# Splitting the first batch's attention into two groups of heads at the start of an attention and feed-forward kernel, with later places for the work behind it

## The chip, the cores and the metric

The kernel runs on one core of a Trainium2 chip. The metric is the device time of one execution in microseconds (us). The kernel before took 573.24 us (median of three runs, 572.38 to 573.35). "TensorE", "VectorE", "ScalarE" are PE, DVE, ACT in the profile; POOL and SP issue the transfers. The kernel's matmuls write to eight PSUM banks, pA0 to pA3 and pF0 to pF3 (pA and pF in the profile).

## The reference

Linformer attention (8 batches, 8 heads, 1024 positions, head size 64), whose keys and values are first projected to 64 rows, then a gated feed-forward part on the 8192 rows that come out.

```python
def _attn_ref(q, k, v, E, F):
    k_proj = np.einsum('ks,bhsd->bhkd', E, k)
    v_proj = np.einsum('ks,bhsd->bhkd', F, v)
    scores = (1.0 / np.sqrt(q.shape[-1])) * np.matmul(q, k_proj.transpose(0, 1, 3, 2))
    # ... softmax over the 64 projected keys ...
    return np.matmul(attn, v_proj)

def _moe_ref(x, w_gate, w_val, w_out):          # x: 8192 x 512
    gate = 1.0 / (1.0 + np.exp(-(x @ w_gate)))   # 512 x 1536
    return gate * (x @ w_val) @ w_out            # 1536 x 512
```

## The kernel before

A small planner (`Plan`) turns the tiles that each operation reads and writes into semaphores. A PSUM bank is one key that every user writes, so any two engines on one bank take turns. `Ring` hands out banks in turn: `whole` has pA0 to pA3 and pF0 to pF2 (used only at the start), `att` pA0 to pA3, `ffn` pF0 to pF3. `mm` is a matmul, `act` a ScalarE operation, `dve` a VectorE one, `busy(n)` issues n small matmuls that only keep TensorE at work ("filler"). Of the tiles, `qT` holds the transposed queries, `kp` and `kpD` the projected keys, `vpD` the projected values, `xT` the attention's output, `hT` the gated values and `ost` the rows on their way out.

The softmax is turned round: exps `eT`, their sums by matmul, a reciprocal on VectorE, a split into two bf16 parts (`rhl`), a broadcast of these by matmul (`bc`, copied to `rb`), and the unnormalised output product (`xo`) multiplied by `rb` into `xT`:

```python
def den():                                   # sums of exps, then VectorE
    bk = ring.next()
    for n in range(4):
        for c in range(4):
            mm(bk, bank[bk][32 * n : 32 * n + 32, 0:P], dsel8[:, n % 2, c, :],
               eT[:, n, c * P : (c + 1) * P], ...)          # (arguments cut)
    dve(lambda e: e.reciprocal(rden[:, 0:P], bank[bk][:, 0:P]), [], [("rden", 0)], b=bk)
    dve(lambda e: e.tensor_copy(rhi[:, 0:P], rden[:, 0:P]), ...)
    dve(lambda e: e.scalar_tensor_tensor(rhl[:, 0:P], ...), ...)
```

The start, on half of batch 0's positions (512 of 1024 make one feed-forward block, and `R` is a group of four heads):

```python
busy(56)
bk = whole.next()
project(0, 0, [bk, bk], 0)          # K
keep_k(bk, 0)
turn_k(whole)
qt, sc, den, bc, xo = half_unit(0, whole)
qt(0); qt(1); sc(0); sc(1)          # (one statement to a line in the kernel)
den()
bks = [whole.next(), whole.next()]
project(1, 1, bks, 0)               # V
keep_v(bks, 0, ["ACT", "DVE", "ACT", "DVE"])
busy(8); bc(0); busy(4); xo(0); bc(1); xo(1); busy(10)
```

Then comes the stream. A block has 12 feed-forward steps (four gate and four value matmuls of 512 columns, then a tanh on ScalarE and `hT` on VectorE), and output products of the block before stand in "gaps". "Step i" below is a place in this list; the first place of block 0 holds the pair of steps 0 and 1. Attention work of later blocks is put into places with `put`:

```python
if blk == 1:
    gaps = {7: [0], 9: [1], 11: [2, 3]}      # output products of block 0
# ...
if b == 0:
    qt, sc, den, bc, xo = half_unit(1, att)  # second half of batch 0
    put(1, lambda: (qt(0), qt(1)))
    put(2, lambda: sc(0))
    put(4, lambda: sc(1))
    put(5, den)
    put(7, lambda: (bc(0), xo(0)))
    put(9, lambda: (bc(1), xo(1)))
    spots = (14, 15, 18, 19, 20, 20, 22, 23, 24, 25)   # attention of batch 1
```

The softmax here doesn't subtract the row's maximum and nothing guards it: scores larger than these inputs give would overflow.

Of the kernel before, what the change touches and what calls it, by code (L numbers as in the profile page):

```python
# [7 lines left out]
ALU = mybir.AluOpType  # L8
# [110 lines left out]
def bass_linformer_attn__then__ffn_glu_sigmoid_kernel(  # L119
# [18 lines left out]
    with contextlib.ExitStack() as es:  # L138
# [94 lines left out]
        def load_k(b):  # L233
            n = 2 * b % 3
            load(
                KV[n][:, :, :],
                k[b].rearrange("h (p t) d -> p h (t d)", t=NT),
                [("KV", n)],
                f"KV{n}",
                r=turned(b - 1) if b >= 2 else (),  # L240
            )

        def load_v(b):
            n = (2 * b + 1) % 3
            load(
                KV[n][:, :, :],
                v[b].rearrange("h (p t) d -> p h (t d)", t=NT),
                [("KV", n)],
                f"KV{n}",
            )  # L250

        def load_q(b):
            s = b % 2
            load(
                Qb[s][:, :, :],
                q[b].rearrange("h (p t) d -> p h (t d)", t=NT),
                [("Q", s, 0), ("Q", s, 1)],
                f"Q{s}",
            )

        def load_q_half(b, hf):
            s, cc = b % 2, slice(256 * hf, 256 * hf + 256)
            load(
                Qb[s][:, :, cc],
                q[b].rearrange("h (p t) d -> p h (t d)", t=NT)[:, :, cc],
                [("Q", s, hf)],
                f"Q{s}{hf}",
            )

        WCH = (0, 256, 512, 1024, 1536)  # L270

        def load_w(j):
            c = slice(WCH[j], WCH[j + 1])
            load(wG[:, :, c], wg_v[:, :, c], [("wG", j)], f"wG{j}")
            load(wV[:, :, c], wv_v[:, :, c], [("wV", j)], f"wV{j}")


        def start_loads():
            for src, rows, n in ((E, slice(0, 64), "E"), (F, slice(64, 128), "F")):
                add(  # L280
                    "SP",
                    lambda e, src=src, rows=rows: e.dma_start(EF[rows, :], src[:, :]),
                    w=[("EF", n)],
                    dma="in" + n,
                )
            for i in range(4):
                pool(
                    lambda e, i=i: e.memset(quad[32 * i : 32 * i + 32, :], 32.0 * i),
                    w=[("quad", i)],
                )  # L290
            load_k(0)
            load_q_half(0, 0)
            load_v(0)
            load_w(0)
            load_w(1)
            load_q_half(0, 1)
            load_w(2)
            load_w(3)

# [119 lines left out]
        def project(n, w, bks, c0):  # L419
            src = KV[n][:, :, :].rearrange("p (r h) (t d) -> p h t r d", h=2, t=NT)  # L420
            for t in range(NT):
                for h in range(2):
                    mm(
                        bks[h],
                        bank[bks[h]][64 * h : 64 * h + 64, c0 : c0 + 256],
                        EFT[:, t, 64 * w : 64 * w + 64],
                        src[:, h, t, :, :],
                        [("KV", n), ("EFT", t // 4)],
# [5 lines left out]
        def keep_k(bk, c0):  # L434
            act(kp[:, :, :], bank[bk][:, c0 : c0 + 256], [], ["kp"], b=bk)

        def keep_v(bks, c0, engines):
            vv = vpD[:, :, :].rearrange("p (r h) d -> p r h d", h=2)
            for n, (h, g) in enumerate(((0, 0), (1, 1), (0, 1), (1, 0))):
                o = vv[64 * g : 64 * g + 64, :, h, :]  # L440
                i = bank[bks[h]][64 * h : 64 * h + 64, c0 : c0 + 256].rearrange(
                    "p (r d) -> p r d", r=NR
                )
                if engines[n] == "ACT":
                    act(o, i, [], [("vpD", h, g)], b=bks[h])
                else:
                    dve(lambda e, o=o, i=i: e.tensor_copy(o, i), [], [("vpD", h, g)], b=bks[h])

        def turn_k(ring):
            bk = ring.next()  # L450
            ob = bank[bk][:, :].bitcast(BF16)
            for r in range(NR):
                for g in range(2):
                    mm(
                        bk,
                        ob[64 * g : 64 * g + 64, r * P : (r + 1) * P],
                        kp[:, r, :],
                        ident[:, :],
                        ["kp", "ident"],
# [4 lines left out]
                kpD[:, :, :].rearrange("p h c -> p (h c)"), ob[:, 0:512], [], ["kpD"], b=bk  # L464
            )

        VPD = [("vpD", h, g) for h in range(2) for g in range(2)]

        def half_unit(hf, ring):
# [4 lines left out]
            def qt(R):  # L474
                bk = ring.next()
                ob = bank[bk][:, :].bitcast(BF16)
                for x in range(4):
                    for t in range(2):
# [6 lines left out]
                            [("Q", s, hf), "ident"],  # L485
# [4 lines left out]
                if R == 0:  # L490
                    dve(lambda e: e.tensor_copy(o, i), [], [("qT", s, hf, R)], b=bk)
                else:
                    act(o, i, [], [("qT", s, hf, R)], b=bk)

            def sc(R):
                bks = [ring.next(), ring.next()]
                for rr in range(2):
                    for c in range(2):
                        h = 4 * R + 2 * rr + c
                        for g in range(2):  # L500
# [6 lines left out]
                                ["kpD", ("qT", s, hf, R)],  # L507
# [13 lines left out]
            def den():  # L521
                bk = ring.next()
                for n in range(4):
                    for c in range(4):
# [11 lines left out]
                    lambda e: e.reciprocal(rden[:, 0:P], bank[bk][:, 0:P]),  # L536
                    [],
                    [("rden", 0)],
# [3 lines left out]
                    lambda e: e.tensor_copy(rhi[:, 0:P], rden[:, 0:P]), [("rden", 0)], ["rhi"]  # L542
# [3 lines left out]
                        rhl[:, 0:P], rhi[:, 0:P], rows[:, 3, 0:1], rden[:, 0:P], ALU.mult, ALU.add  # L546
                    ),
                    [("rden", 0), "rhi", "rows"],
                    ["rhl"],
                )  # L550

            def bc(R):
                bks = [ring.next(), ring.next()]
                for c in range(4):
                    for g in range(2):
# [7 lines left out]
                            ["bsel8", "rhl"],  # L563
# [7 lines left out]
            def xo(R):  # L571
                bks = [ring.next(), ring.next()]
                for rr in range(2):
                    for g in range(2):
                        for c in range(2):
# [7 lines left out]
                                VPD + [("eT", 2 * R + g)],  # L583
# [18 lines left out]
        def transpose_q(b):  # L602
            s = b % 2
            for r in range(NR):
# [6 lines left out]
                    r=[("Q", s, 0), ("Q", s, 1)],  # L611
                    w=[("qT", s, r), ("qT", s, 0, r // 2), ("qT", s, 1, r // 2)],
# [3 lines left out]
        def attention(b):  # L616
            s = b % 2

            def kv():
# [7 lines left out]
                for t in range(NT):  # L627
                    for w in range(2):
# [7 lines left out]
                            [("KV", n), ("EFT", t // 4)],  # L636
# [14 lines left out]
                for g in range(2):  # L651
# [4 lines left out]
                        [("vpD", h, g) for h in range(2)],  # L656
# [3 lines left out]
            def turn_kd():  # L660
                if b == 1:
# [9 lines left out]
                    w=["kpD"],  # L671
# [3 lines left out]
            def sc(r2):  # L675
                for r in (2 * r2, 2 * r2 + 1):
                    bks = [att.next(), att.next()]
                    for c in range(2):
                        h = 2 * r + c
                        for g in range(2):  # L680
# [6 lines left out]
                                ["kpD", ("qT", s, r)],  # L687
# [13 lines left out]
            def den():  # L701
# [14 lines left out]
                for c in range(4):  # L716
# [4 lines left out]
                        [("rden", c)],  # L721
# [3 lines left out]
            def split():  # L725
                rd = [("rden", c) for c in range(4)]
                dve(lambda e: e.tensor_copy(rhi[:, :], rden[:, :]), rd, ["rhi"])  # L727
# [4 lines left out]
                    rd + ["rhi", "rows"],  # L732
                    ["rhl"],
                )

            def bc(rnd):
                for j in range(4):
# [6 lines left out]
                        ["bsel", "rhl"],  # L744
# [4 lines left out]
            def gather():  # L749
                for i in range(4):  # L750
# [3 lines left out]
                        r=[("rden", c) for c in range(4)],  # L754
# [16 lines left out]
            def xo(r2):  # L771
                for r in (2 * r2, 2 * r2 + 1):
                    bks = [att.next(), att.next()]
                    for g in range(2):
                        n = 2 * r + g
                        for c in range(2):
# [6 lines left out]
                                VPD + [("eT", n)],  # L783
# [32 lines left out]
        def msteps(blk, ms):  # L816
            s, hf = (blk // 2) % 2, blk % 2
            pbs = {}
            for m in ms:
                for n in "GV":  # L820
                    pbs[m, n] = ffn.next()
            for i in range(NI):
                for m in ms:
                    j = max(x for x in range(4) if WCH[x] <= m * P)
                    for n, W in (("G", wG), ("V", wV)):
                        if len(ms) > 1:
                            mm_one(blk, m, j, i, n, W, pbs[m, n], s, hf)
            if len(ms) == 1:
                m = ms[0]
                j = max(x for x in range(4) if WCH[x] <= m * P)  # L830
                for n, W in (("G", wG), ("V", wV)):
                    for i in range(NI):
                        mm_one(blk, m, j, i, n, W, pbs[m, n], s, hf)
            for m in ms:
                gate(blk, m, pbs[m, "G"], pbs[m, "V"])

        def mm_one(blk, m, j, i, n, W, pb, s, hf):
# [5 lines left out]
                [("w" + n, j), ("xT", s, i, hf, 0), ("xT", s, i, hf, 1)],  # L843
# [55 lines left out]
        busy(56)  # L899
        bk = whole.next()  # L900
        project(0, 0, [bk, bk], 0)
        keep_k(bk, 0)
        turn_k(whole)
        qt, sc, den, bc, xo = half_unit(0, whole)
        qt(0)
        qt(1)
        sc(0)
        sc(1)
        den()
        bks = [whole.next(), whole.next()]  # L910
        project(1, 1, bks, 0)
        keep_v(bks, 0, ["ACT", "DVE", "ACT", "DVE"])
        busy(8)
        bc(0)
        busy(4)
        xo(0)
        bc(1)
        xo(1)
        busy(10)
# [4 lines left out]
        load(wO[:, :, :], moe_w_out.rearrange("(m p) c -> p m c", p=P), ["wO"], "wO")  # L924
# [7 lines left out]
        for b in range(B):  # L932
            todo = []
            for blk in (2 * b, 2 * b + 1):
# [3 lines left out]
                if blk == 1:  # L938
                    gaps = {7: [0], 9: [1], 11: [2, 3]}
                else:  # L940
                    gaps = {2: [0], 5: [1], 8: [2], 11: [3]}
                for m in ms:
                    todo.append(lambda blk=blk, m=m: msteps(blk, m))
# [8 lines left out]
            if b == 0:  # L952
                qt, sc, den, bc, xo = half_unit(1, att)
                put(1, lambda: (qt(0), qt(1)))
                put(2, lambda: sc(0))
                put(4, lambda: sc(1))
                put(5, den)
                put(7, lambda: (bc(0), xo(0)))
                put(9, lambda: (bc(1), xo(1)))
                spots = (14, 15, 18, 19, 20, 20, 22, 23, 24, 25)  # L960
# [10 lines left out]
            if b == 0:  # L971
                put(3, lambda: transpose_q(1))
                put(15, lambda: load_next(2))
# [43 lines left out]
```

## Time and profile before

The time is fixed by when the steady stream of feed-forward matmuls starts and by each later moment at which TensorE waits (it is busy for 97% of the span). So I cut the trace of the kernel before at four points, all starts of TensorE groups in the timeline:

| point | start, us |
|---|---|
| the mark: gate matmuls of the third step of block 0 | 29.38 |
| first gate matmuls of block 1 (B1G) | 50.46 |
| first value matmuls of block 1 (B1V) | 51.33 |
| first gate matmuls of block 2 (B2) | 89.97 |
| span | 570.5 |

After B2 the programs are the same, so a difference of two kernels is the sum of the differences of these stretches.

### The profile page before, as it was taken

Reading aid. Unit: us, or ns where it says so; the run is one execution under the profiler, and the core shown is the slowest. Engines: PE = TensorE matmul, PEld = TensorE weight load, DVE = VectorE, ACT = ScalarE, POOL = GpSimd, SP = SyncE. Lnnn points to the kernel's source line nnn. Section 1 sums busy time; section 2 is a strip of 40 time slices with the busy share of each in tenths; the row PEclk is TensorE's granted clock in tenths of the full one; section 3 lists DMA queues with packets and bytes.
Section 4 is the critical chain, followed back from the end, with each engine's and each line's share of the span. In section 5 each row is a group of like instructions: output and inputs, shape, how many; then the busy total and the mean of one; then the engine's idle time right before and its main releaser. Section 6 shows DMA issues by size and latency. Waiting matters only on the chain.

```text
span 570.5 us, 7585 instructions
## 1 busy us (share of the span) xinstructions
PE 552.1 (97%) x2960; PEld 248.6 (44%) x3014; DVE 247.8 (43%) x392; ACT 175.7 (31%) x305; POOL 100.4 (18%) x138
## 2 busy tenths in 40 slices
PE   5799999999999999999999999999999999999997
PEld 5444434444444444444444444444444444444443
DVE  4345265334633536235543355334462354533332
ACT  2454551442233322342123422243213332222220
POOL 8100010106300081002700044000700007000000
PEclk9999999999999999999999999999999999999999
DMA  9999899984755059521687037660411101010012
GB/s 160 200 207 201 121 185 147 182 159 77 139 112 98 33 113 165 98 61 51 109 158 120 19 79 126 133 102 37 80 52 47 37 22 39 37 38 27 30 37 92
DMA packets 74212, 56.00 MB, mean 98 GB/s; under 512 B 34528, under 2 KB 65760, under 8 KB 74176
## 3 DMA queue, kind: packets, MB, share of 16 engines
q0 software_dynamic: 31776, 29.89, 34.3%
q1 hardware_dynamic: 42400, 25.63, 18.3%
q8 instruction: 23, 0.38, 0.3%
q14 instruction: 13, 0.11, 0.1%
HBM read 60.29 MB, written 16.78 MB: 135 GB/s over the span
## 4 chain that ended last, share of the span: by engine, by line
PE 85%; DMA 10%; POOL 2%; DVE 1%; issue 1%; SPq 0%; ACT 0%; DVEq 0%; POOLq 0%
PE pF L210 78%; PE pA L210 7%; DMA Qb<-in_q_dram 6%; DMA qT<-Qb 4%; DVE rden L719 1%; POOL wG L228 1%; POOL wV L228 1%; POOL KV L228 0%; POOL Qb L228 0%; SPq L607 0%; DVE rhl L729 0%; DVE ost L882 0%; DVE hT L855 0%; ACT sig L214 0%; DVE rhi L727 0%
## 5 line engine op out<-in xcount | busy, mean ns | idle before, releaser
L855 DVE SCALAR_TENSOR_TENSOR hT<-sig,pF 128x512 bf16<-128x512 f32 x192 | 130.6, 685 | 203.5 <-PE pF L210 153.5
L214 ACT ACTIVATE sig<-pF 128x512 f32<-128x512 f32 x192 | 114.3, 599 | 315.7 <-PE pF L210 312.8
L210 PE MATMUL pF<-xT,wV 128*128 128x512 bf16 x754 | 196.7, 379 | 1.6 <-DVE xT L589 0.9
L210 PE MATMUL pF<-xT,wG 128*128 128x512 bf16 x747 | 194.5, 379 | 2.3 <-issue 1.4
L210 PE MATMUL pF<-wO,hT 128*128 128x512 bf16 x702 | 163.5, 379 | 1.5 <-issue 0.8
L210 PEld LDWEIGHTS pF<-xT,wV 128*128 128x128 bf16 x768 | 75.2, 98 | 90.8 <-issue 0.6
L210 PEld LDWEIGHTS pF<-xT,wG 128*128 128x128 bf16 x768 | 72.2, 98 | 95.3 <-issue 12.9
L764 POOL PARTITION_BROADCAST rb<-rrow x96 | 70.8, 798 | 212.8 <-DMA rrow<-rden 207.7
L210 PEld LDWEIGHTS pF<-wO,hT 128*128 128x128 bf16 x720 | 69.3, 98 | 87.2 <-issue 5.8
L882 DVE TENSOR_SCALAR ost<-pF 128x512 f32<-128x512 f32 x60 | 41.5, 691 | 94.0 <-PE pF L210 94.0
L214 ACT ACTIVATE eT<-pA 128x512 bf16<-128x512 f32 x63 | 32.7, 603 | 10.2 <-PE pA L210 10.2
L789 DVE TENSOR_TENSOR xT<-pA,rb 128x512 bf16<-128x512 f32 x56 | 34.7, 681 | 0.0
L719 DVE RECIPROCAL rden<-pA 128x128 f32<-128x128 f32 x28 | 23.7, 910 | 0.0
L228 POOL DMA_DIRECT2D KV<-in_k_dram x8 | 7.3, 918 | 87.9 <-PE pA L210 56.3
L228 POOL DMA_DIRECT2D KV<-in_v_dram x8 | 7.1, 882 | 80.5 <-PE pF L210 79.1
L214 ACT ACTIVATE kpd<-pA 64x1024 bf16<-64x1024 f32 x6 | 6.1, 1017 | 28.3 <-PE pA L210 28.3
L210 PE MATMUL pA<-KV,EFT 128*64 128x512 bf16 (+1 forms) x144 | 14.5, 346 | 0.0
L210 PE MATMUL pA<-qT,kpD 64*64 64x512 bf16 (+1 forms) x140 | 10.6, 367 | 0.4 <-ACT qT L214 0.3
L210 PE MATMUL pA<-wO,hT 128*128 128x512 bf16 x47 | 10.5, 379 | 0.1
L210 PE MATMUL pA<-eT,vpD 64*64 64x512 bf16 (+1 forms) x136 | 10.4, 370 | 0.0
L210 PEld LDWEIGHTS pA<-KV,EFT 128*64 128x64 bf16 x144 | 7.4, 109 | 6.8 <-issue 3.0
L214 ACT ACTIVATE rb<-pA 128x512 f32<-128x512 f32 x14 | 7.5, 617 | 4.9 <-PE pA L210 4.9
(67 smaller groups left out, 104.4 us busy)
## 6 DMA issues: line engine op xcount, KB each, us to landing
out_dram<-ost SPq DMA_DIRECT2D x64, 256.0 KB, 2.0
KV<-in_k_dram POOLq DMA_DIRECT2D x8, 1024.0 KB, 10.4
KV<-in_v_dram POOLq DMA_DIRECT2D x8, 1024.0 KB, 14.6
Qb<-in_q_dram POOLq DMA_DIRECT2D x7, 1024.0 KB, 15.0
wO<-in_moe_w_out_dram POOLq DMA_DIRECT2D x1, 1536.0 KB, 49.6
Qb<-in_q_dram POOLq DMA_DIRECT2D x2, 512.0 KB, 17.1
wG<-in_moe_w_gate_dram POOLq DMA_DIRECT2D x2, 512.0 KB, 25.2
wV<-in_moe_w_val_dram POOLq DMA_DIRECT2D x2, 512.0 KB, 27.0
```

Of the source, the lines that this page charges most:

```text
L210: return add("PE", lambda e: e.matmul(o, lhsT, rhs, **kw), r=r, x=[("bank", b)])
L214: return add("ACT", lambda e: e.activation(o, i, func, scale=scale), r=r, w=w, x=x)
L228: add("POOL", lambda e: e.dma_start(o, i), r=r, w=w, dma=sem)
L719: lambda e, cc=cc: e.reciprocal(rden[:, cc], bank[bk][:, cc]),
L764: lambda e, n=n, i=2 * rnd + c, j=j, parts=parts: e.partition_broadcast(rb[0:parts, n, :], rrow[32 * j : 32 * j + 1, i, :], channels=parts),
L789: lambda e, r=r, g=g, n=n, bk=bks[g]: e.tensor_tensor(xT[s][:, r, :, 256 * g : 256 * g + 256], bank[bk][:, :].rearrange("p (f c) -> p f c" ...
L855: lambda e: e.scalar_tensor_tensor(hT[blk % 2][:, m, :], sg[:, :], 1.0, bank[pv][:, :], ALU.add, ALU.mult,),
L882: lambda e: e.tensor_scalar(o[:, :], bank[pb][:, :], 0.5, None, op0=ALU.mult),
```

## The change

Its intent is to begin sooner: load K, Q and V of batch 0 by groups of four heads, and finish the first group's attention and half of the first feed-forward pair while the second group is still on its way. With it go later places for the second half of batch 0 and for batch 1, all output products of block 0 at the end of block 1, and a wait of the output weights' load for the transposed queries of batch 1. Core of the diff:

```diff
-            load_k(0)
-            load_q_half(0, 0)
-            load_v(0)
-            load_w(0)
+            for R in range(2):
+                load_kv_heads(0, k, R)
+            for R in range(2):
+                load_q_half(0, 0, R)
+            for R in range(2):
+                load_kv_heads(1, v, R)
+            load_w(0, 0)
+            load_w(0, 1)
 ... (weights in more, smaller pieces; keys by group of heads; den, sc, xo per group)
-        busy(56)
 ... (the start as shown above)
+        busy(40)
 ... (one line: half_unit)
+        for R in range(2):
+            bk = whole.next()
+            project(0, 0, [bk, bk], 0, R)
+            busy(4)
+            keep_k(bk, 0, R)
+            turn_k(whole, R)
+            busy(8)
+        qt(0, ("DVE", "ACT"))
+        busy(6)
+        sc(0)
+        qt(1, ("DVE", "DVE"))
+        busy(6)
+        den(0)
+        sc(1)
+        busy(4)
 ... (v_part(R, ring): the V projection of group R on two banks of the ring, and its copies to vpD)
+        bc(0)
+        den(1)
+        v_part(0, whole)
+        busy(4)
+        bc(1)
+        xo(0)
+        busy(8)
+        for _ in range(-att.turn % 4):
+            att.next()
+        v_part(1, att)
 ... (first pair: matmuls i=0,1 of step 0, then xo(1), i=0,1 of step 1, then i=2,3)
+        transpose_q(1)
         load(wO ...
+            r=turned(1),
-                    gaps = {7: [0], 9: [1], 11: [2, 3]}
+                    gaps = {11: [0, 1, 2, 3]}
-                put(1, lambda: (qt(0), qt(1)))
 ... (places 1, 2, 4, 5, 7, 9 as shown above)
+                put(5, lambda: (qt(0, ("DVE", "ACT")), qt(1, ("DVE", "ACT"))))
+                put(6, lambda: sc(0))
+                put(7, lambda: (den(0), sc(1)))
+                put(8, lambda: (den(1), bc(0)))
+                put(9, lambda: (xo(0), bc(1)))
+                put(10, lambda: xo(1))
-                spots = (14, 15, 18, 19, 20, 20, 22, 23, 24, 25)
+                spots = (16, 17, 18, 19, 20, 20, 22, 23, 24, 25)
```

## The prediction

> **What bounds the kernel now.** I read the page first (busy shares and the 40 slices), then the timeline of the first 110 us, then the chain of work and the landings of the loads. The page says that this is a TensorE kernel from the third slice on, at full clock, with nothing else near its limit:
>
> ```profile
> PE 552.1 (97%) x2960; PEld 248.6 (44%) x3014; DVE 247.8 (43%) x392; ACT 175.7 (31%) x305; POOL 100.4 (18%) x138
> ...
> PE   5799999999999999999999999999999999999997
> ...
> PEclk9999999999999999999999999999999999999999
> ```
>
> So the time is the start of the steady stream of feed-forward matmuls, plus TensorE work that the change doesn't alter, plus every later moment at which TensorE waits. The change touches only the first 100 us; a microsecond won or lost there is one in the end. The timeline shows how the stream starts (columns: start, time, engine, line, operation, out<-in, idle before):
>
> ```profile
> 19.52 0.96 DVE L536 RECIPROCAL rden<-pA 128x128 f32<-128x128 f32 x1 [3.23 <-PE pA L210]
> ...
> 20.74 1.06 PE L210 MATMUL pF<-KV,EFT 128*64 128x256 bf16 x16 [1.25 <-DMA KV<-in_v_dram]
> 20.78 0.35 DVE L545 SCALAR_TENSOR_TENSOR rhl<-rhi,rows,rden 128x128 bf16<-128x128 bf16 x1
> ...
> 23.52 1.29 DVE L589 TENSOR_TENSOR xT<-pA,rb 128x512 bf16<-128x512 f32 x2 [0.76 <-PE pF L210]
> ...
> 24.72 1.28 DVE L589 TENSOR_TENSOR xT<-pF,rb 128x512 bf16<-128x512 f32 x2
> ...
> 26.06 0.39 PE L210 MATMUL pF<-xT,wG 128*128 128x512 bf16 x1
> ...
> 29.38 1.02 PE L210 MATMUL pF<-xT,wG 128*128 128x512 bf16 x4
> ```
>
> The load of v is waited for until 20.74. But rhl (the inverse of the sums) is ready only at 21.13, and from there a chain through VectorE runs: vpD (two copies from 21.87, 0.89 together) until 22.76, then the four xT products until 26.00. The first pair's remaining 14 matmuls run from 26.06 at 0.216 us each, and the next step starts at 29.38. **That 29.38 is the mark** that I carry over.
>
> After it TensorE is full but for two waits:
>
> ```profile
> 67.42 3.05 DMA qT<-Qb
> ...
> 73.83 3.31 DVE rden L719 x4
> ...
> 77.62 0.76 DVE rhl L729
> ```
>
> Those are pieces of the chain of work (start, time, what). The timeline has the two TensorE groups:
>
> ```profile
> 70.05 0.96 PE L210 MATMUL pA<-qT,kpD 64*64 64x512 bf16 x8
> ...
> 78.44 0.39 PE L210 MATMUL pA<-rhl,bsel 32*128 32x512 bf16 x4 [0.62 <-DVE rhl L729]
> ```
>
> The chain says that the last transpose of batch 1's queries lands at 70.47, and the second score group takes 0.96 us where the first took 0.63: about 0.35 us of waiting. And 0.62 us is lost on the four reciprocals and the split of batch 1.
>
> [...] I expect a granted clock of 1.0 again. [...] a query transpose takes 11.87 and 10.22 us beside the loads and 3.05 us alone. [...]
>
> **The change, part by part.**
>
> *Loads.* The bytes ahead of each need hardly change. K lands at 12.2 now (issue 1.34 plus 10.9), Q's half at 14.3, V at 20.6. In the new order the first half of K comes about 2 to 3 us before, the first half of V at about 18 (0.5 MB at 0.2 MB/us before 20.6). More issues at 0.73 us apart stay ahead of the data. Every weight chunk lands before its matmuls need it.
>
> *Head, group 0.* The filler shrinks from 56 to 40, at 0.093 us each, so projection starts at 11.0 instead of 12.44. But there are now two rounds of project (0.6), copy (0.27), turn (0.3), copy (0.38) with fillers between: the queries are turned at 14.75, qT's halves are ready at 15.8 (VectorE, half of 0.69) and 16.45 (ScalarE after it), and the first scores end at 16.9, as before. Exps until 18.06, sums of two groups instead of four, reciprocal at 18.55 (before 19.52), rhl at 20.15: **1.0 us earlier**.
>
> *Head, group 1.* The broadcast of group 0 stands ahead of the sums of group 1 in TensorE's order and waits for rhl (20.3). So the second reciprocal starts at 20.95; 0.96 + 0.23 + 0.35 plus gaps gives rhl of group 1 at 22.55. A reciprocal of 64 partitions costs what one of 128 does[...]. The two VectorE copies of vpD stand behind it[...]: 22.6 to 23.2, against 22.76 before. xT of group 0: 23.8 to 25.1, against 24.81. The second V projection takes the attention banks pA0 and pA1, and pA0 is freed only by that xT: it starts at 25.2. First four feed-forward matmuls 25.7 to 26.5; vpD of group 1 at 26.5; the output product at 26.6; xT of group 1 from 27.1 to 28.4; the eight left matmuls from 28.5 take 1.73 us. Mark: **30.2 against 29.38, +0.8 us**. Starting half of the pair early doesn't repay, for VectorE's chain ends 2.4 us later and only six fewer matmuls (1.3 us) and a bank wait (0.3) stand behind it.
>
> *Second half of batch 0.* Its products now run in the steps 5 to 10 of block 0, not 1 to 9, and the last output product stands directly before block 1. Its third matmul needs that xT. In steady state an hT starts 0.28 us after the last V matmul is issued and takes 0.69, then two xT at 0.65: 2.3 us, plus 0.1 to be seen. TensorE has only the product (0.35) and two matmuls (0.43) to do meanwhile. **+1.5 us**, a wait that wasn't there. Broadcast 0 now has one step (1.73 us) after its sums, not two, and VectorE needs hT, reciprocal, two small ones: about 2.45. **+0.1 us**.
>
> *Batch 1.* All output products of block 0 go to the end of block 1, so between sums and broadcast stand two steps (3.46 us) where a step and an output product stood (4.33). The VectorE chain is the same (from 72.77 to 78.39). The wait of 0.62 grows by 0.87, and a bit more as ScalarE has less time for its exps: **+1.0 us**.
>
> *Output weights.* Without them beside the transposes, the latter should land by about 65 rather than 70.5; the scores need them at about 69 and 71. **-0.35 us**. The weights then land at about 76; the first output product is at about 80. No wait, but the margin is 4 us.
>
> Sum: 0.8 + 1.5 + 0.1 + 1.0 - 0.35 = **+3.05**, so 576.3 from the median; as the head is the part I trust least and splitting may have been tuned by its writer, I put 576.0.
>
> **Rivals.** (a) *The head gains.* If the whole head is bound by the loads (the wait on v speaks for it), halving them lets the stream start 1 to 2 us sooner: 571 to 573, with the waits in batch 0 and 1 smaller than I count. Against: rhl and VectorE end later than v already. (b) *The output weights come late.* If the transposes stay at 70, the weights land above 80 and each us is lost: 577 to 580. For: the margin is small, and K and V of batch 1 still run beside the transposes. Against: alone a transpose takes 3 us. (c) *All is hidden*: VectorE is used 43%, so the waits may be filled: 573. Against: order on TensorE is fixed, nothing can fill them.
>
> **Range and chances.** My terms are good to about 0.7 us for the head, 0.4 for each wait; (a) pulls 3 us down, (b) 2 up. Range 572.8 to 578.2. Two per cent are 11.5 us, which needs something that I don't see, such as a stalled queue: faster 0.01, same 0.96, slower 0.03.
>
> **What would show it.** Right: the 1.02 us group of step 2 near 30.2; rhl twice, near 20.15 and 22.55; the second V projection waiting on xT, not on a load; a wait of about 1.5 us on xT at the first step of block 1 (near 50); the wait on rhl near 79 grown to about 1.6; no wait on wO. Wrong: the mark under 28.5, a wait on a DMA of V or of a weight, or PE waiting on wO near 80.

That the clock would be 1.0 again was my estimate; the trace of the kernel before has a mean granted clock of 1.000. That the copies of `vpD` stand behind the second reciprocal follows from the order of work on VectorE. The trace of before shows such an order: the tanh of the step at 73.32 ends at 75.05, and its `hT` starts at 78.29, behind the four reciprocals and the split, which run from 73.74 to 78.37. TensorE shows it too: the eight fillers at 21.74, which read nothing of v, stand behind the V projection that waited 1.25 us for it. That a reciprocal of 64 partitions costs what one of 128 does was an estimate too; the changed kernel has 0.95 and 0.96 us. For the transposes, "beside the loads" is 199 GB/s (44 to 55 us of the trace of before), "alone" 0 GB/s (66 to 68.5).

## The result and the profile after

The changed kernel took **575.70 us** (median of four runs, 575.25 to 576.88) against 572.81 us (four runs, 572.19 to 573.35) on the same chip. The ratio is 1.0054, with a 95% interval of 1.0033 to 1.0075. A ratio here is the mean time of one kernel's fast runs over that of the other's of the same rounds, so it is not quite the ratio of the quoted medians. The interval lies wholly above 1: the change costs about half a per cent. All outputs are right.

The page of the changed kernel (busy time by engine, then TensorE and its granted clock in 40 slices) looks like the one before:

```profile
PE 556.9 (97%) x3060; PEld 248.8 (43%) x3060; DVE 251.5 (44%) x403; ACT 176.2 (31%) x310; POOL 107.2 (19%) x148
...
PE   5799989999999999999999999999999999999997
...
PEclk9999999999999999999999999999999999999999
```

The busy sums of TensorE can't be compared, since the trace before lacks some records (2960 of its matmuls are there). The sixth slice (72 to 86 us) has an 8 where before it had a 9, and no clock is lost in this execution (mean granted clock 1.000). The stretches tell where the time went:

| stretch | before | after | difference | predicted |
|---|---|---|---|---|
| start to mark | 29.38 | 30.55 | +1.17 | +0.8 |
| mark to B1G | 21.08 | 21.39 | +0.31 | +0.1 |
| B1G to B1V | 0.87 | 2.22 | +1.35 | +1.5 |
| B1V to B2 | 38.64 | 38.76 | +0.12 | +1.0 - 0.35 |
| sum | 89.97 | 92.92 | +2.95 | +3.05 |

The spans of the two profiled executions are 570.5 and 573.4 us, so this is the whole difference.

**The start.** The timeline of the changed kernel (columns: start, time, engine, line, operation, out<-in, count, idle before):

```profile
18.42 0.95 DVE L583 RECIPROCAL rden<-pA 64x128 f32<-64x128 f32 x1 [0.32 <-PE pA L210]
...
19.71 0.34 DVE L594 SCALAR_TENSOR_TENSOR rhl<-rhi,rows,rden 64x128 bf16<-64x128 bf16 x1
...
21.01 0.96 DVE L583 RECIPROCAL rden<-pA 64x128 f32<-64x128 f32 x1 [0.95 <-PE pA L210]
...
22.27 0.35 DVE L594 SCALAR_TENSOR_TENSOR rhl<-rhi,rows,rden 64x128 bf16<-64x128 bf16 x1
...
22.54 0.62 DVE L485 CAST vpD<-pA 64x128 bf16<-64x128 f32 x2
...
24.45 0.68 DVE L639 TENSOR_TENSOR xT<-pA,rb 128x512 bf16<-128x512 f32 x1
...
25.28 0.64 PE L210 MATMUL pA<-KV,EFT 128*64 128x128 bf16 x16 [1.02 <-DVE xT L639]
...
27.39 1.29 DVE L639 TENSOR_TENSOR xT<-pA,rb 128x512 bf16<-128x512 f32 x2 [0.72 <-PE pA L210]
...
28.82 0.59 PE L210 MATMUL pF<-xT,wG 128*128 128x512 bf16 x2 [0.63 <-DVE xT L639]
...
30.55 1.03 PE L210 MATMUL pF<-xT,wG 128*128 128x512 bf16 x4
```

The first group does get ready sooner: its `rhl` ends at 20.05, where the one `rhl` of before ended at 21.13. But the second group needs a reciprocal of its own, which takes 0.96 us for 64 partitions, as the one for 128 did, and whose sums stand behind the first group's broadcast in TensorE's order (at 20.44, where the broadcast waited for `rhl` until 20.11). From its end at 21.97 everything is later than before: the `vpD` copies, the second V projection, which waits 1.02 us until the first group's `xT` gives a bank back, and the last `xT`, which ends at 28.68 instead of 26.00. No load is waited for any longer in this part; VectorE's order has taken the load's place.

**The second half of batch 0.** At the first step of block 1, before and then after:

```profile
50.46 1.03 PE L210 MATMUL pF<-xT,wG 128*128 128x512 bf16 x4
...
51.33 1.03 PE L210 MATMUL pF<-xT,wV 128*128 128x512 bf16 x4
```

```profile
51.94 0.61 PE L210 MATMUL pF<-xT,wG 128*128 128x512 bf16 x2
...
53.71 0.60 PE L210 MATMUL pF<-xT,wG 128*128 128x512 bf16 x2 [1.17 <-DVE xT L639]
...
54.16 1.03 PE L210 MATMUL pF<-xT,wV 128*128 128x512 bf16 x4
```

Four matmuls became two and two, with a wait on `xT` between: the output product that makes it stands directly ahead.

**Batch 1.** Before, then after, from the scores to B2:

```profile
80.59 0.77 PE L210 MATMUL pA<-rhl,bsel 32*128 32x512 bf16 x4
...
84.50 2.48 DVE L789 TENSOR_TENSOR xT<-pA,rb 128x512 bf16<-128x512 f32 x4
...
86.45 0.98 PE L210 MATMUL pA<-eT,vpD 64*64 64x512 bf16 x8
...
89.97 1.03 PE L210 MATMUL pF<-xT,wG 128*128 128x512 bf16 x4
```

```profile
72.01 0.64 PE L210 MATMUL pA<-qT,kpD 64*64 64x512 bf16 x8
...
75.77 3.38 DVE L769 RECIPROCAL rden<-pA 128x128 f32<-128x128 f32 x4
...
80.46 0.40 PE L210 MATMUL pA<-rhl,bsel 32*128 32x512 bf16 x4 [1.82 <-DVE rhl L780]
...
83.49 0.40 PE L210 MATMUL pA<-rhl,bsel 32*128 32x512 bf16 x4
...
87.22 2.47 DVE L840 TENSOR_TENSOR xT<-pA,rb 128x512 bf16<-128x512 f32 x4
...
89.76 0.63 PE L210 MATMUL pA<-eT,vpD 64*64 64x512 bf16 x8
...
92.92 1.03 PE L210 MATMUL pF<-xT,wG 128*128 128x512 bf16 x4
```

The wait on `rhl` grew from 0.62 to 1.82, that is by 1.20. But three groups became shorter: the second scores (0.96 to 0.64), the second broadcast (0.77 to 0.40) and the second output product (0.98 to 0.63), together by 1.04. That leaves 0.16, and the stretch shows 0.12. These groups of before had waits inside them, which the timeline prints as idle time of the weight loads and not of the matmuls: 0.41 us in the second scores (weight loads at 70.57, where the last transpose lands at 70.47), 0.28 on `rb` in the second broadcast (80.97), 0.44 on `xT` in the second output product (87.03).

Two of these inner waits are for banks, and the timeline shows why they went. The second broadcast needs the banks that ScalarE's four copies of the first (`rb`) still read: before, these ended at 80.92, after its start at 80.59; now they end at 82.94 and it starts at 83.49, for a whole product stands between the broadcasts, and not a step. The second output product (`xo`) needs the banks that the four `xT` of the first still read. One product of block 0 stands between the two in both kernels (3.33 and 3.25 us from start to start); what changed is the work ahead of the first. Before, that was a step, and VectorE did its `hT` (at 83.89) before it began the `xT`, 1.38 us after the first product's start, so that they ended at 86.98, after 86.45. Now they begin 0.71 us after it and end at 89.69, before 89.76.

**The output weights.** Their load, issued by POOL, waits for the transposed queries:

```profile
60.17 1.01 POOL L228 DMA_DIRECT2D wO<-in_moe_w_out_dram  x1 [39.67 <-DMA qT<-Qb]
```

The view of the transfers gives 13.0 us to landing, so they are there at about 73.2, and the first product that needs them starts at 80.79. No wait.

### The profile page after: what moved, and what is told of

It is laid out like the page before. It is cut to its first block, busy times and chain, and to the rows that moved or that the text cites. A ratio compares the mean times of both kernels' runs of the same rounds, so it can differ in the third digit from the quotient of the medians.

```text
span 573.4 us, 7766 instructions
## 1 busy us (share of the span) xinstructions
PE 556.9 (97%) x3060; PEld 248.8 (43%) x3060; DVE 251.5 (44%) x403; ACT 176.2 (31%) x310; POOL 107.2 (19%) x148
## 4 chain that ended last, share of the span: by engine, by line
PE 95%; DVE 3%; ACT 1%; issue 0%; DVEq 0%
PE pF L210 86%; PE pA L210 9%; ACT eT L214 1%; DVE rden L769 1%; DVE xT L639 0%; DVE rden L583 0%; DVE count L327 0%; DVE hT L910 0%; DVE dsel L388 0%; ACT sig L214 0%; DVE rhl L780 0%; DVE rhl L594 0%; DVE ost L937 0%; ACT qT L214 0%; ACT kp L214 0%
## 5 line engine op out<-in xcount | busy, mean ns | idle before, releaser
L210 PE MATMUL pF<-xT,wG 128*128 128x512 bf16 x768 | 198.3, 379 | 1.8 <-DVE xT L639 1.8
L210 PE MATMUL pF<-wO,hT 128*128 128x512 bf16 x732 | 168.1, 379 | 0.0
L210 PE MATMUL pA<-KV,EFT 128*64 128x512 bf16 (+2 forms) x176 | 15.4, 319 | 1.0 <-DVE xT L639 1.0
L214 ACT ACTIVATE vpD<-pA 64x512 bf16<-64x512 f32 (+2 forms) x20 | 9.7, 484 | 2.2 <-PE pA L210 1.8
L228 POOL DMA_DIRECT2D Qb<-in_q_dram x11 | 9.4, 866 | 0.0
```

The costliest lines, as they stand in the source:

```text
L210: return add("PE", lambda e: e.matmul(o, lhsT, rhs, **kw), r=r, x=[("bank", b)])
L214: return add("ACT", lambda e: e.activation(o, i, func, scale=scale), r=r, w=w, x=x)
L228: add("POOL", lambda e: e.dma_start(o, i), r=r, w=w, dma=sem)
```

## The experiments

All twelve ran with five rounds, so that each kernel has six executions. Some executions have a mean granted clock of 0.99 to 0.997, others 0.999 or more. I call the former **cold** and the latter **warm**. Of the 33 executions of the kernel before 12 were warm (median 572.33) and 21 cold (573.49). The changed kernel was measured twice (the result above and e12_change_again): four of those ten executions were warm (median 575.34) and six cold (577.1). So the ratios of the runs mix two things, and I read each mechanism from a stretch of the trace and use times of warm runs beside it. The three calls ran on three chips; the warm medians of the kernel before in them are 572.26, 572.58 and 572.25, so a difference of 0.3 us between calls says little.

| run | median (range), us | ratio [95%] | warm runs |
|---|---|---|---|
| e1_slots | 575.71 (573.89 to 576.74) | 1.0044 [1.0026, 1.0062] | 2 of 6: 573.89, 573.91 |
| e2_kv_early | 576.35 (575.08 to 578.04) | 1.0062 [1.0044, 1.0080] | 3 of 6, median 575.15 |
| e3_banks | 575.88 (574.79 to 576.98) | 1.0058 [1.0042, 1.0074] | 1 of 6: 574.79 |
| e4_sums_first | 575.17 (573.92 to 576.77) | 1.0040 [1.0023, 1.0057] | 5 of 6, median 575.17 |
| e9_products_between | 575.99 (574.59 to 577.17) | 1.0046 [1.0028, 1.0065] | 1 of 6: 574.59 |
| e7_old_head | 574.07 (573.37 to 575.13) | 1.0014 [0.9997, 1.0031] | 4 of 6, median 574.04 |
| e6_wo_at_once | 576.79 (575.23 to 578.21) | 1.0052 [1.0027, 1.0076] | 2 of 6: 575.23, 575.27 |
| e12_change_again | 577.13 (575.40 to 578.20) | 1.0066 [1.0041, 1.0090] | 1 of 6: 575.40 |
| e10_filler | 575.28 (574.38 to 575.49) | 1.0027 [1.0011, 1.0043] | 6 of 6 |
| e8_old_filler | 572.34 (571.77 to 574.24) | 0.9987 [0.9964, 1.0010] | 5 of 6, median 572.22 |
| e5_all | 572.03 (571.75 to 573.69) | 0.9981 [0.9963, 0.9999] | 6 of 6 |
| e11_best | 572.90 (571.70 to 573.07) | 0.9990 [0.9969, 1.0011] | 6 of 6 |

### The wait on xT: one step earlier

```diff
-                put(5, lambda: (qt(0, ("DVE", "ACT")), qt(1, ("DVE", "ACT"))))
+                put(4, lambda: (qt(0, ("DVE", "ACT")), qt(1, ("DVE", "ACT"))))
 ... (6 to 5, 7 to 6, 8 to 7, 9 to 8 likewise)
-                put(10, lambda: xo(1))
+                put(9, lambda: xo(1))
```

> The changed kernel with the second half of batch 0 one step earlier (steps 4 to 9 of block 0, not 5 to 10), so that a whole step of 1.73 us stands between its last output product and block 1. My theory (TensorE waits for VectorE's last xT there): the wait of 1.17 us before the third matmul of block 1 is gone, from the mark (third step of block 0) to the first V matmul of block 1 the stretch shrinks by some 1.3 us, and the time is 1.2 to 1.4 us under the changed kernel's 575.7, so 574.4. Rival (the wait only moves, for VectorE is behind at this point and the next step waits instead): under 0.4 us less, and a new wait on VectorE near 50 us.

In its timeline the first step of block 1 is whole again:

```profile
53.95 1.03 PE L210 MATMUL pF<-xT,wG 128*128 128x512 bf16 x4
...
54.81 1.03 PE L210 MATMUL pF<-xT,wV 128*128 128x512 bf16 x4
```

Its mark is at 32.55, so mark to B1V is 22.26 against 23.61 in the changed kernel: 1.35 less, the whole of this term. The two warm executions have a span of 572.1 against 573.4. So this cause is shown. The profiled execution was cold, and its windows of one microsecond show what that is (columns: window, its length, busy share and count of PE, PEld, DVE, ACT, POOL, then the granted clock, DMA share and GB/s):

```profile
19.00:20.00 1.00, 0.68 (x13) 0.30 (x12) 0.95 (x1) 0.53 (x2) 1.00 (x2) 1.00 1.45 194
20.00:21.00 1.00, 0.01 (x2) 0.01 (x2) 0.87 (x2) 0.55 (x2) 0.51 (x1) 1.00 1.44 194
...
22.00:23.00 1.00, 1.00 (x20) 0.83 (x14) 0.96 (x2) 0.74 (x3) 0.00 (x0) 0.50 1.46 197
...
29.00:30.00 1.00, 1.00 (x12) 0.31 (x4) 0.60 (x1) 0.00 (x0) 0.00 (x0) 1.00 1.50 210
```

The clock is halved from about 21.5 to 28.4 (worked out from the mean clocks of the windows in which it changes, 0.77 and 0.81), for 6.8 us. In the last three whole windows before the drop (18 to 21 us) TensorE was idle for 44% (busy for 0.98, 0.68 and 0.01 us), though never for longer than 1.5 us at once. The cold profiles of e2_kv_early (19 to 22) and e4_sums_first (22 to 25), read alike, give 46% and 44%, and half clock for 6.8 us (22.9 to 29.7) and 3.4 us (25.2 to 28.6). But what share suffices these runs don't show: the changed kernel's profiled execution was idle for 55% from 22 to 25 us and kept a clock of 1.00.

### Batch 1 one step earlier

```diff
-                spots = (16, 17, 18, 19, 20, 20, 22, 23, 24, 25)
+                spots = (15, 16, 17, 18, 19, 19, 22, 23, 24, 25)
```

> The changed kernel with batch 1's first parts (projection, turning, both score groups, sums) one step earlier each, the broadcast where it is: three steps (5.2 us) between sums and broadcast, not two (3.5 us). My theory (the wait of 1.82 us on rhl is VectorE's chain of four reciprocals, 5.6 us, against the steps that stand between): wait about 0.1 us, time 1.7 us under 575.7, so 574.0. Rival (the wait of batch 1 is really for the transposed queries or for v, which come late): the wait reappears at the scores or the projection as a wait on a DMA, and the time stays within 0.4 us of 575.7.

This puts a whole step more between sums and broadcast. The wait on `rhl` did go, and came back as another:

```profile
75.71 3.38 DVE L769 RECIPROCAL rden<-pA 128x128 f32<-128x128 f32 x4
...
80.26 1.28 DVE L910 SCALAR_TENSOR_TENSOR hT<-sig,pF 128x512 bf16<-128x512 f32 x2
...
81.00 1.04 PE L210 MATMUL pF<-xT,wV 128*128 128x512 bf16 x4 [1.55 <-DVE hT L910]
```

B1V to B2 is 38.60 against 38.76, so only 0.16 was won. My theory, that the broadcast comes too soon after the sums, fell. VectorE runs four reciprocals (3.38 us) and the split in order (75.71 to 80.34), and a feed-forward step needs VectorE too, to empty its bank: the two `hT` come only at 80.26. A further step didn't cover VectorE's chain: it waited 1.55 us for it.

### Output products between sums and broadcast

```diff
-                    gaps = {11: [0, 1, 2, 3]}
+                    gaps = {9: [0, 1], 11: [2, 3]}
```

> The changed kernel with two of block 0's output products moved from the end of block 1 to behind its tenth step, so that between the sums of batch 1 and their broadcast stand two products (5.4 us) which need no hT of VectorE, where two steps (3.5 us) stood that do. After the run that put the sums earlier only moved the wait onto hT: my new theory is that VectorE's chain of 4.6 us blocks every step behind it by order, so that only work without VectorE hides it. Expected: the wait on rhl is under 0.2 us, no wait on hT takes its place, the stretch from the first V matmul of block 1 to block 2 falls from 38.8 to 37.1 us, time 1.6 us less at the same clock. Rival (the output weights, which land near 73, or the ring of banks make TensorE wait instead): a wait on the weights or on ost of over 1 us.

An output product is twelve matmuls that need VectorE only at their end. Two of them now stand beside the reciprocals:

```profile
80.72 0.40 PE L210 MATMUL pA<-rhl,bsel 32*128 32x512 bf16 x4
...
82.88 0.76 PE L210 MATMUL pA<-rhl,bsel 32*128 32x512 bf16 x4
...
88.74 0.98 PE L210 MATMUL pA<-eT,vpD 64*64 64x512 bf16 x8
```

The wait on `rhl` is gone. B1V to B2 is 37.84, 0.92 less, not the 1.7 less that I expected (37.1): the second broadcast and the second output product are long again, at the lengths that they had before the change. So the same two products can cover the reciprocals, or stand ahead of the second broadcast and of the first output product in place of steps, but not both. This also shows what the prediction had missed in batch 1.

### The bank of the second V projection

```diff
-        for _ in range(-att.turn % 4):
+        for _ in range(-att.turn % 4 + 2):
```

> The changed kernel with the second v projection of the head on the banks pA2 and pA3 and its output product on pA0 and pA1, the other way round than now; nothing else. My theory (the projection at 25.28 us waits 1.02 us only because xT of group 0 still reads pA0): the projection starts near 24.3, the mark comes at 29.9 rather than 30.55, and the time is 0.6 us under 575.7. Rival (the head is bound by VectorE's own string of work, whatever the banks): the projection starts earlier, but the last xT and the mark move by under 0.2 us.

The projection takes pA2 and pA3, which are free, and no longer waits:

```profile
24.38 0.64 PE L210 MATMUL pA<-KV,EFT 128*64 128x128 bf16 x16
```

From the first query transposes to the mark it takes 15.16 us (14.94 to 30.10) against 15.86 (14.69 to 30.55): 0.70 less, where 0.65 was expected. Of the times only one is warm, 574.79: it lies 0.55 below the changed kernel's warm median, where 0.6 was expected, but one execution is thin evidence.

### Sums of the second group ahead of the first group's broadcast

```diff
-        bc(0)
         den(1)
         v_part(0, whole)
+        bc(0)
```

> The changed kernel with the sums of group 1 issued ahead of the broadcast of group 0 in the head; nothing else. My theory (the second reciprocal at 21.01 waits for sums that stand behind a broadcast that itself waits for the first rhl): second reciprocal near 20.2, second rhl ready near 21.9 rather than 22.62, mark 0.6 to 0.7 us earlier, time 0.6 us under 575.7. Rival (the exps on ScalarE or the load of v set the pace of group 1): the second rhl moves by under 0.2 us, and the mark stays.

From the first query transposes to the second V projection it takes 9.99 us (15.42 to 25.41) against 10.59 (14.69 to 25.28): 0.60 less. In order, the broadcast held the second group's sums back until the first `rhl` was there. The warm median, 575.17, is only 0.17 below that of the changed kernel, less than the trace gives; two of its executions, at 573.92 and 574.35, are lower. Nor can this trace show the gain at the mark, for its clock was halved from 25.2 to 28.6 us (granted clock 0.58, 0.50, 0.50 and 0.71 in the four windows from 25 us). The run with all mends, below, can.

### The head of before with the later schedule

```diff
 (kernel before)
+        transpose_q(1)
-        load(wO[:, :, :], moe_w_out.rearrange("(m p) c -> p m c", p=P), ["wO"], "wO")
+        load(wO[:, :, :], moe_w_out.rearrange("(m p) c -> p m c", p=P), ["wO"], "wO", r=turned(1))
-                    gaps = {7: [0], 9: [1], 11: [2, 3]}
+                    gaps = {11: [0, 1, 2, 3]}
 ... (steps 5 to 10 and the spots of the changed kernel, den() whole, load_next(2) at 17)
```

> The kernel before with only the later part of the change: batch 0's second half in steps 5 to 10, all products of block 0 at the end of block 1, batch 1's parts where the change puts them, the output weights behind the transposed queries; the head is the old one, not split. My theory (head and later schedule cost separately): mark as in the kernel before (29.4), first V of block 1 23.3 us after it (before 21.95), then 38.8 us to block 2 (before 38.6): 1.5 us slower than before, 574.3. Rival (the later schedule was made for the split head and its split sums, and without it costs more, or the head is what costs all): 575.5 or more, or 572.8.

This does all of the change but the split and its smaller loads. Warm runs have a median of 574.04, against 574.3 expected; the warm ones of the kernel before in the same call have 572.58. So the schedule alone costs about 1.5 us and the split the other 1.3 (575.34 less 574.04). In the trace mark to B1V is 23.50, with 1.38 us of waiting on `xT`, and B1V to B2 is 38.76, with 1.81 on `rhl`: both about as in the changed kernel, so neither wait comes from the split. Mark to B1G is 21.08, as before the change, so the 0.31 there does come from it: this run keeps the sums of the second half whole. The mark itself, expected at 29.4, is at 30.57, because the profiled execution was cold (mean granted clock 0.66 from 20 to 25 us); that the old head loses nothing is read from the warm times, which are 1.46 over the kernel before where the two stretches alone give 1.67.

### The output weights at once

```diff
-            r=turned(1),
```

> The changed kernel without the wait of the output weights' load for the transposed queries: it is issued at once, behind the loads of batch 1, as before. My theory: the transposes land near 71 again, not near 60; in the changed order their scores are issued near 69.6 and 72.0, so the wait is 0 to 0.8 us there, and the time goes up by no more than that (575.7 to 576.5). Rival (the delayed load is what saves the schedule): the scores wait 2 us or more; other rival (it never mattered): no wait at all.

The two warm executions have 575.23 and 575.27, where the changed kernel has 575.34. Mark to B2 is 62.37 in both traces (33.51 to 95.88, and 30.55 to 92.92). The issues of the four transposes now stretch over 18.7 us instead of 13.0, but the second scores take 0.64, as in the changed kernel: in the new schedule they are needed late enough anyway. So the wait for the transposes buys nothing here. One caution: the profiled execution was cold (granted clock 0.58 from 20 to 25 us, 0.50 from 25 to 30, 0.89 from 30 to 35) and 3 us late at the mark, which gave the transposes that much more time; the warm times are the better evidence.

### The change again, unchanged

No edit.

> The changed kernel itself once more, for its rate of clock drops and as the yardstick of the runs beside it. My theory (in its head TensorE idles a little more than in the kernel before's, so that the clock falls in some executions of both): executions at a mean clock of 0.999 or more near 575.2, those under it 1 to 2 us longer; the best execution of the changed kernel 2.5 to 3 us above the best of the kernel before. Rival (the loss is the clock's, not the schedule's): the undisturbed executions of the two kernels lie within 1 us of each other.

The ratio is 1.0066, with 1 of 6 executions warm. The warm one, 575.40, agrees with the first measurement; the cold ones lie between 576.04 and 578.20. The warm runs of the two kernels are 3.0 us apart (575.34 and 572.33 over all calls), as much as the two traces at full clock, so the rival that the loss is the clock's fell. How often an execution falls cold differs from call to call, and it moves a median by more than most of these experiments do.

### More filler

```diff
         sc(1)
-        busy(4)
+        busy(16)
 ...
         v_part(0, whole)
-        busy(4)
+        busy(14)
         bc(1)
         xo(0)
-        busy(8)
+        busy(20)
```

> The changed kernel with 34 more filler matmuls in the head (12 before the first broadcast, 10 before the second, 12 before the second v projection), each set shorter than the wait that stands there (0.7, 0.6 and 0.7 us in waits of 1.06, 0.93 and 1.02). Found in the runs so far: in some executions the granted clock falls to 0.5 for some 7 us between 20 and 30 us. My theory [...]: with the filler every execution shows a mean clock of 0.999 to 1.0, the executions agree within 1.2 us, and the median is 0.3 to 1 us under the changed kernel's 575.7. Rival (the drops have nothing to do with the program's gaps): as many drops as in the other runs, about half, and no gain.

What was left to test is whether the drops come from TensorE's idle time in the head. With filler in the gaps all six executions are warm, within 1.1 us of each other, where four of the changed kernel's ten were. Filler didn't make the kernel quicker than its own warm runs (575.28 against 575.34); in these six the cold ones are gone. The same in the kernel before:

```diff
 (kernel before)
         den()
+        busy(16)
 ...
         xo(1)
-        busy(10)
+        busy(18)
```

> The kernel before with 16 filler matmuls in its wait for v and 8 more ahead of the first pair, nothing else. My theory (its own executions with clock drops, about half, cost it 1 to 2 us each): all executions at a mean clock of 0.999 or more, median near 572.2, spread under 1 us, no faster than its best executions now (572.0). Rival (its drops come from elsewhere): as many drops.

Five of six are warm, with a median of 572.22. The cold one is the profiled one: there the clock fell before the new filler, which starts at 21.26 (mean granted clock 0.55 from 15 to 20 us, 0.77 from 20 to 25), and after a wait of 1.9 us for K. The ratio's interval holds 1.

### All mends together

```diff
 (e1_slots, e3_banks, e4_sums_first and e9_products_between together, and)
-        busy(4)
+        busy(8)
 ...
-        busy(4)
+        busy(10)
 ...
         v_part(1, att)
+        busy(4)
```

> The changed kernel with all that I hold for repairs: second half of batch 0 one step earlier, second v projection on free banks, sums of group 1 ahead of the broadcast, two products between the sums and the broadcast of batch 1, a little filler in the gaps. My theory says the parts add: -1.3, -0.65, -0.6 and -1.7 against the changed kernel, so 571.4 at full clock, about 1.4 under the kernel before. Rival (each repair only uncovers the next wait in VectorE's order): no better than 573.

The median is 572.03, where 571.4 was expected, the ratio 0.9981 [0.9963, 0.9999]. This is 3.3 us below the changed kernel's warm runs. Against the kernel before it is not a win that I would claim: all six executions were warm, while 8 of the 11 of the kernel before were cold. Its warm median is 572.33, and the two differ by 0.3 us. Its head takes 14.63 us from the first query transposes to the mark (14.86 to 29.49), 1.23 less than the changed kernel's 15.86: the bank's 0.70 and the sums' 0.60 nearly add. In the trace the mark is at 29.49 (29.38 before), B1V at 51.75 (51.33), B2 at 91.33 (89.97). From B1V to B2 it would be ahead but for a new wait, since everything came earlier but the output weights did not:

```profile
74.52 5.35 PE L210 MATMUL pF<-wO,hT 128*128 128x512 bf16 x24 [1.83 <-DMA wO<-in_moe_w_out_dram]
```

So I moved these two products one step later:

```diff
-                    gaps = {9: [0, 1], 11: [2, 3]}
+                    gaps = {10: [0, 1], 11: [2, 3]}
```

> The run with all repairs, but the two output products one step later (behind the eleventh step of block 1), so that the output weights, which kept TensorE waiting 1.83 us there, have landed. My theory: no wait on the weights, a wait on rhl of about 0.6 us as in the kernel before (a step and a product between sums and broadcast), some 1.0 us under the run with all repairs: 571.0, about 1.5 to 2 us under the kernel before and 1 us under the kernel before with filler. Rival (the step that now stands behind the sums loses on hT what the weights' wait gave): 572 or more.

It missed: 572.90, not 571.0. In its trace the wait on the weights is gone and B2 is at 90.15, but part of the wait on `rhl` is back:

```profile
78.04 0.39 PE L210 MATMUL pA<-rhl,bsel 32*128 32x512 bf16 x4 [0.95 <-DVE rhl L780]
```

The profiled execution of e5_all was its slowest (573.69), while four of its others lie between 571.75 and 572.20. So the wait of 1.83 us may be peculiar to that execution. In e11_best it is the traced execution that is among the quickest (572.48). Only one execution of each kernel is traced, and whether the weights come in time in the others stays open.

## Why the prediction was right or wrong

The direction and the size were right: 576.0 predicted, 575.70 measured. The sum of the steps (+3.05) met the +2.95 of the traces, but partly because errors cancelled: that it fits this closely is luck.

- **What bounds the kernel: too broad.** "Nothing else near its limit" holds for the other engines. The DMA row of the same page, which the prediction doesn't show, has 8 or 9 tenths in the first nine slices (to 128 us), so by that row the transfers were busy nearly all through the part that was changed. No load is waited for in the new head, so this did not spoil the sum.

- **Head, group 0: right.** `rhl` 20.15 foretold, 20.05 measured; the filler's and projections' times were good enough. The halves of qT did come one after the other on their bank (VectorE from 15.34 to 15.76, ScalarE from 15.80).
- **Head, group 1: right in mechanism, too small.** Foretold and measured: second reciprocal 20.95 and 21.01, `rhl` 22.55 and 22.62, `xT` from 23.8 and 23.84, second V projection 25.2 and 25.28, output product 26.6 and 26.82, last `xT` to 28.4 and 28.68, mark 30.2 and 30.55. The mis-sized term is "+0.8", which measured +1.17: small delays at each handover add up in a serial chain. e3_banks and e4_sums_first show two of its waits apart, at 0.70 and 0.60 us, e5_all shows that mending both brings the mark back to 29.49, and the warm times of e7_old_head, without the split, leave no room for this loss.
- **Second half of batch 0: right.** "+1.5" measured +1.35, and e1_slots takes exactly that away. "+0.1" at the broadcast was wrong: there is no wait. In its place the stretch grew by 0.31, for two sums of eight matmuls took 0.34 each where one of sixteen took 0.37; I had not counted the split there (e7_old_head, with whole sums, has 21.08 as before).
- **Batch 1: the wait right, the net wrong.** "+1.0" measured +1.20. But the prediction took the four products at the end as only a loss. They also take the place of the steps between the two broadcasts and ahead of the first output product (`xo`), which removed 0.37 and 0.35 us of waits for banks inside the second broadcast and the second `xo`. e9_products_between, which moves two products back, brings both back. So the term is +0.12 in place of +0.65.
- **Output weights: the sign right, the credit misplaced.** The second scores did lose their 0.32 us of waiting. The transposes were over at 60.2, not 65, and the weights there at 73.2, not 76. But e6_wo_at_once shows no gain from the wait itself, so the later places of the scores suffice for it. (That a transpose is slower beside the loads shows in the trace of before: 11.87 and 10.22 us against 3.05.)
- **The clock: true of the profiled run, not in general.** "I expect a granted clock of 1.0 again" held in the first set's profile. Across the two sets of the changed kernel six of ten executions were below 0.999, at a cost of about 2 us (medians 577.1 and 575.34). That TensorE's gaps are short did not keep the clock up: in e1_slots it halved with no gap over 1.5 us in the windows before.
- **The rivals.** That the head gains was false (the mark is 1.17 later), that the weights come late was false in the changed kernel (it did happen in e5_all), and that all is hidden was false.

## What to carry to other kernels

Splitting a serial chain into groups shortens the first group, but each group pays the fixed operations again (a reciprocal of 64 partitions took 0.95 and 0.96 us, one of 128 took 0.96), and the second stands behind the first in an engine's order (here its sums, at 20.44, behind a broadcast that waited until 20.11); count when the last group ends, not the first. Cover a long VectorE chain with matmuls that don't need VectorE (in e9_products_between that took away a wait of 1.82 us, though other waits came back), and put a whole step between a product and the block that reads its result (1.35 us in e1_slots). Where TensorE idles in pieces at a start, check the granted clock of many executions, not of one (six of the changed kernel's ten were cold, by 1.8 us in the median).
